# Attention and token mixer in one kernel: order of the last projection tiles, place of the row statistics, and a planner's weights

## The chip, the cores and the metric

The kernel runs on one core of a Trainium2 chip. The metric is the device time of one execution in microseconds (us). An execution that the hardware profiler recorded gives the trace; its own time is stated beside the others.

## The reference

```
x = A_x                                            # (1, 2048, 512)
g = sigmoid((x * gate_w).sum(-1, keepdims=True))
q, k, v = split of x @ wqkv into 32 heads of 16
a = softmax(q k^T * 16**-0.5) v, heads joined, @ wo
h = layernorm(x)                                   # over the 512 channels
u = gelu(h^T w1 + b1)                              # over the 2048 tokens: (512, 1792)
b = (u w2 + b2)^T                                  # (2048, 512)
return g * a + (1 - g) * b
```

All inputs and the output are float32.

## The kernel before, in words

**Products in three parts.** A float32 factor is split into a high and a low part of TensorE's reduced float32 format; a product is three matmuls (high by high, high by low, low by high). A projection tile of 512 tokens by 128 columns, or of 128 tokens by 512 columns of v, has 512 rows of weights, four blocks of 128, and so twelve matmuls of 128 x 512.

**Tiles of q and k.** There are 32 tiles, numbered T: four of 512 tokens for each block of 128 columns, key block 0 (T 0 to 3), query block 0 (T 4 to 7), key block 1 (T 8 to 11), and so on. A tile is copied from its PSUM bank to `qraw`, cut into its parts in a buffer named `pc` (a key tile two parts, a query tile three, the third with a bound of the scores), and its parts are stored to DRAM (`kp`, `qp`), all in `qk_parts`. The greatest absolute value of its columns is kept besides. For a group (a pair of heads and half of the queries) the parts are loaded back as stacks of rows: `load_k` (six transfers to `ks`, for half of the keys) and `load_q` (eight transfers to `qs`). Query tiles 4 and 5 hold the first half of the queries of block 0.

**The first stage** loads x, turns it (by TensorE for the first four row blocks of 128 tokens, by VectorE from blocks `xb` for the rest), and multiplies v tile by tile. `order` lists its v tiles as numbers and the tiles 0 to 5 of k and q as strings ("woven" among them); at place i of `order` the lists `calls`, `cuts` and `stats` say what else is issued: loads, stores, and `row_stats(t)`, which gives mean, variance and the gate's sum of 128 tokens. `last` holds what is left of the woven tile before: low part, greatest value, third part and store. `store_v` writes v to DRAM for later groups. The two `pc` buffers of this stage serve the woven tiles in turn.

**The hand-over.** Tiles 6, 7 and 8 are then multiplied alone (`tile_alone`), each in one of seven PSUM banks named `s`; the eighth bank is `dn`. With them come, on ScalarE and VectorE, the layer norm's 1 / deviation (`rs`) and the gate (`g`, `omg`) of all tokens, with a load of the activation tables for the square root and one for the exponential. A first phase of eight scores follows (`mixed`): four, tile 9 alone, four. Then the phases of twelve scores begin, the first with tile 10 alone ahead of it.

**Phases.** A score is a matmul of 64 x 128 by 64 x 512 to one bank. In a phase, scores on one half of TensorE's rows stand beside matmuls on the other half, which add up a tile of q or k (or, in the second attention part, of the mixer's second layer) in `dn`. ScalarE takes exponentials of one or two banks to `pt`; four banks of each phase are first copied to `quad` by VectorE (line 779 of the kernel before) and have one exponential together. At a phase's end the exponentials of the phase before are multiplied with v (line 839).

**The plan of banks.** `plan_banks` decides, when the program is built, in which bank each score goes. It walks the phases with estimates of each engine's time, keeps the eight best states (`WIDTH`), and orders them by `State.worth`. `kept` holds a neighbouring bank for the second score of a pair that has one exponential, with the time from which it is free. There are two plans: the mixed phase with the 42 phases of twelve scores of the first attention part, and the second attention part.

All engines' instructions stand in the order in which the code issues them, but for small moves that the scheduler makes; all transfers are issued by one queue, SP's, in order. A transfer waits until the eighth before it has landed.

Of the kernel before, what the change touches and what calls it, by code (L numbers as in the profile page):

```python
# [22 lines left out]
P = 128  # L23
# [53 lines left out]
def gated_mix(ctx: ExitStack, tc: tile.TileContext, a_x, a_wqkv, a_wo, b_w1, b_b1, b_w2, b_b2, gate_w, out):  # L77
# [129 lines left out]

    def qk_parts(T, raw, pc, alone):

        j, b, is_q, n = qk_tile(T)  # L210
        low, high = (2, 0) if is_q else (1, 0)
        if n == 0:
            (qmax if is_q else kmax)[b] = small.tile([P, NQ], F32, name="qmax" if is_q else "kmax")
# [11 lines left out]
        def first():  # L225
            (nc.scalar.copy if alone else nc.vector.tensor_copy)(pc[:, high, :], raw)

        def second():
            nc.vector.tensor_tensor(pc[:, low, :], raw, pc[:, high, :].bitcast(F32), ALU.subtract)

        def shift():
            if alone:
                nc.scalar.activation(pc[:, 1, :], raw, AF.Abs, scale=kmax[b][:, 0:1])
            else:
                most_k, other = kmax[b][:, 0:1], pc[:, 1, :].bitcast(F32)
                nc.vector.tensor_scalar(pc[:, 1, :], raw, most_k, -1.0, ALU.mult, ALU.mult)
                nc.vector.scalar_tensor_tensor(pc[:, 1, :], raw, most_k, other, ALU.mult, ALU.max)

        def store():
            dst = (qp_d if is_q else kp_d)[b]  # L240
            nc.sync.dma_start(dst[:, :, n * NB : (n + 1) * NB].rearrange("c p t -> p c t"), pc.bitcast(F32))

        return [(0.45, first), (0.7, greatest), (0.7, second), *([(1.2, shift)] if is_q else [])], store

    def parts_of(pool, T, **kw):
        return pool.tile([P, 3, NB], F32R, name="pc", **kw)[:, : 3 if qk_tile(T)[2] else 2, :]

# [21 lines left out]
    with tc.tile_pool(name="vp", bufs=1, side="right") as pool:  # L269
# [32 lines left out]
        blocks_of = {}  # L302

        def load_blocks(t):
            blocks_of[t] = pool.tile([P, QUARTERS, P], F32, name="xb", bufs=4)
# [37 lines left out]
        def store_v(t, to):  # L343
            nc.sync.dma_start(v_d[:, t:to], v[:, t:to])
# [4 lines left out]
        with tc.manual_schedule():  # L349
# [70 lines left out]
            def woven(T):  # L420
# [17 lines left out]
            def v_tile(t):  # L438
# [15 lines left out]
            cuts, late_cuts = {}, []  # L454
            stats = {**{i: [i] for i in range(10)}, 13: [10], 14: [11], 15: [12], 16: [13], 17: [14], 18: [15]}
            for i, what in enumerate(order):
# [16 lines left out]
                for call in calls.get(i, ()):  # L473
# [8 lines left out]
            store_v(12, NS)  # L482
            load_q(0)
    acc_ctx.close()
# [34 lines left out]
    TILES_PT, QUADS = 8, 2  # L519
    WIDTH = 8  # L520

# [6 lines left out]
    class State:  # L528

        def __init__(self, free):  # L530
            self.free = list(free)
# [58 lines left out]
        def score(self, n, ops, parked, u, bank, since, alone):  # L590
# [4 lines left out]
            if alone:  # L595
                at = min(range(RING), key=lambda b: new.free[b])
                new.pe = max(new.pe + TURN, new.free[at]) + ALONE_PE + TURN
                new.act = max(new.act, new.pe) + ALONE_ACT
                new.free[at] = new.act
                new.alone += ((u, at),)  # L600
# [80 lines left out]
        def worth(self):  # L681
            return self.pe + 0.02 * sum(max(0, f - self.pe) for f in self.free) + 0.1 * max(0, self.act - self.pe)

    def plan_banks(phases, free):

        best = [State(free)]
        sets = 0
# [12 lines left out]
        best = sorted((new for old in best for new in old.with_v(0, (), (), 0.0, sets)), key=State.worth)  # L700
        log, steps, free = best[0].log, [], best[0].free
# [4 lines left out]
        return deque(step[1:] for step in reversed(steps) if step[0] == "s"), v_banks, free  # L706

# [259 lines left out]
    with tc.manual_schedule(engines=engines):  # L967
        e, y, t_, w_ = (small.tile([P, NS], F32, name=f"st{n}", bufs=1) for n in range(4))
        turn_of = deque(range(RING))

        def tile_alone(T, bank):
            for n, (a, b) in enumerate(qk_pairs(T)):
                writes(nc.tensor.matmul(banks[:, bank, :], a, b, start=n == 0, stop=n == 3 * ND - 1), bank)  # L973
            raw = qe.tile([P, NB], F32, name="qraw", bufs=4)
            reads(nc.scalar.copy(raw, banks[:, bank, :]), bank)  # L975
            steps, store = qk_parts(T, raw, parts_of(qe, T, bufs=4), T < ALONE - 1)
            for n in (0, 2, 3, 1):
                if n < len(steps):
                    steps[n][1]()
            store()  # L980

        for T in range(WOVEN, ALONE - 2):
# [5 lines left out]
            tile_alone(T, turn_of[0])  # L988
            if T == WOVEN:
                nc.vector.tensor_scalar_add(w_, mv[:, :, 1], EPS)  # L990
                nc.scalar.activation(y, w_, AF.Sqrt)
                nc.scalar.activation(e, z, AF.Exp, scale=-1.0)
                nc.vector.tensor_scalar_add(e, e, 1.0)
                nc.vector.reciprocal(g, e)
                nc.vector.tensor_scalar(omg, g, -0.5, 0.5, ALU.mult, ALU.add)
            if T == WOVEN + 1:
                nc.vector.reciprocal(y, y)
                nc.vector.tensor_mul(t_, y, y)
                nc.vector.tensor_mul(t_, t_, w_)
                nc.vector.tensor_scalar(t_, t_, -0.5, 1.5, ALU.mult, ALU.add)  # L1000
                nc.vector.tensor_mul(rs, y, t_)
            if T < WOVEN + 2:
# [555 lines left out]
```

## Time and profile before

| what | value |
|---|---|
| time, median of three executions | 1256.97 us |
| the three executions | 1256.45, 1256.97, 1263.55 us |
| time of the profiled execution | 1262.87 us |
| its span, first to last instruction | 1260.0 us |
| TensorE (PE) busy | 1243.1 us, 99% |
| ScalarE (ACT) busy | 1079.3 us, 86% |
| VectorE (DVE) busy | 776.1 us, 62% |
| GpSimd (POOL) busy | 215.8 us, 17% |
| mean granted TensorE clock | 0.992 |
| first attention part, from its first score to the mixer's first layer | 78.72 to 334.94 us |
| mixer's first layer, up to the first score of the second part | to 491.87 us |

The waits of an engine are grouped by the line that waited and the instruction that ended the wait; after the colon stand the total in us, how many, and the longest. In a timeline a row is the start, the length, the engine, the line, and what is written from what; a number in brackets is the idle time ahead of it. In a table by stretches, the clock that TensorE was granted, the share of the DMA engines and GB/s stand last.

### The profile page before, as it was taken

The numbers are of one execution on the slowest core, as the hardware profiler recorded it, in microseconds if no ns is written. First come the engines' busy times: TensorE is split into PE (matmuls) and PEld (weight loads), VectorE is DVE, ScalarE is ACT, GpSimd is POOL, SyncE is SP. The second block draws the span as 40 slices with busy tenths as digits, with TensorE's granted clock in tenths as the row PEclk, the third lists the DMA queues.
The fourth block names the chain that finished last, engine by engine and source line by source line (L and its number), as shares of the span: only waits on it lengthen the run. The fifth ranks groups of instructions, "written<-read, shape, count | busy, mean of one in ns | idle before, by whom it ended". The sixth has DMA issues, their size and how long they took to land.

```text
span 1260.0 us, 33250 instructions
## 1 busy us (share of the span) xinstructions
PE 1243.1 (99%) x13446; PEld 798.8 (63%) x13446; DVE 776.1 (62%) x1318; ACT 1079.3 (86%) x1561; POOL 215.8 (17%) x345
## 2 busy tenths in 40 slices
PE   9989999999999999999999999999999999999998
PEld 7865666666678886566566556655666566555666
DVE  6747887888784347555455445545555556647974
ACT  4459999999734337999999999999999999999990
POOL 5400000000145444111111111101112111100000
PEclk9989999999999999999999999999999999999999
DMA  6882544452464433054234333324433443436642
GB/s 184 284 255 70 135 121 129 111 154 94 125 211 134 123 100 106 23 127 94 73 78 104 95 86 92 92 68 101 106 82 92 107 127 94 105 73 177 180 135 88
DMA packets 169919, 149.17 MB, mean 118 GB/s; under 512 B 82055, under 2 KB 127261, under 8 KB 169374
## 3 DMA queue, kind: packets, MB, share of 16 engines
q1 hardware_dynamic: 169758, 146.97, 42.9%
q8 instruction: 108, 1.77, 0.6%
q14 instruction: 53, 0.43, 0.1%
HBM read 108.50 MB, written 38.39 MB: 117 GB/s over the span
## 4 chain that ended last, share of the span: by engine, by line
PE 95%; ACT 2%; DMA 1%; DVE 1%; issue 0%; SPq 0%; ACTq 0%; DVEq 0%
PE s L839 36%; PE s L789 34%; PE s L1215 12%; PE dn L803 5%; PE acc L91 3%; PE pa L1434 2%; PE acc L424 1%; PE s L973 1%; DMA row<-bp 1%; ACT pt L772 1%; DMA x<-in_A_x_dram 0%; PE acc L388 0%; DVE quad L779 0%; PE dn L1434 0%; ACT qraw L975 0%
## 5 line engine op out<-in xcount | busy, mean ns | idle before, releaser
L772 ACT ACTIVATE pt<-s 128x512 f32<-128x512 f32 (+1 forms) x1217 | 717.3, 704 | 5.8 <-PE s L789 3.1
L789 PE MATMUL s<-qs,ks 64*128 64x512 f32 x2048 | 526.8, 404 | 9.1 <-DVE quad L779 2.9
L789 PEld LDWEIGHTS s<-qs,ks 64*128 64x128 f32 x2048 | 353.0, 185 | 170.6 <-ACT pt L772 74.2
L779 DVE COPY quad<-s 128x512 f32<-128x512 f32 x616 | 401.1, 687 | 52.1 <-PE dn L803 35.2
L839 PE MATMUL s<-pt,vt 128*17 128x256 f32 x5728 | 422.5, 380 | 0.0
L768 ACT ACTIVATE quad<-quad 128x2048 f32<-128x2048 f32 x154 | 300.3, 1950 | 1.3 <-DVE quad L779 1.2
L839 PEld LDWEIGHTS s<-pt,vt 128*17 128x17 f32 x5728 | 181.2, 97 | 164.9 <-ACT pt L772 53.3
L851 DVE TENSOR_TENSOR ot<-s,ot 128x256 f32<-128x256 f32 (+1 forms) x155 | 79.4, 512 | 304.6 <-PE s L839 212.9
L803 PE MATMUL dn<-u,w_hi 64*128 64x512 f32 x768 | 256.5, 407 | 0.0
L839 PE MATMUL s<-quad,vt 128*17 128x256 f32 x2464 | 226.6, 379 | 0.0
L1042 POOL TENSOR_TENSOR w_lo<-w_raw,w_hi 128x512 fp32r<-128x512 f32 (+1 forms) x127 | 149.6, 1183 | 101.6 <-ACT w_hi L1039 78.3
L808 POOL MEMSET token<- 1x1 f32 x154 | 18.0, 117 | 849.9 <-PE dn L803 772.5
L803 PE MATMUL dn<-u,w_lo 64*128 64x512 f32 x384 | 156.1, 406 | 0.0
L839 PEld LDWEIGHTS s<-quad,vt 128*17 128x17 f32 x2464 | 100.7, 98 | 60.2
L803 PEld LDWEIGHTS dn<-u,w_hi 64*128 64x128 f32 x768 | 136.5, 185 | 2.3 <-POOL token L808 0.2
L1215 PE MATMUL s<-h,w_hi 128*128 128x512 f32 x392 | 121.0, 390 | 0.0
L1039 ACT CAST w_hi<-w_raw 128x512 fp32r<-128x512 f32 (+1 forms) x64 | 36.1, 565 | 58.4 <-PE s L1215 30.3
L1215 PEld LDWEIGHTS s<-h,w_hi 128*128 128x128 f32 x392 | 73.5, 188 | 15.7 <-issue 0.4
L1215 PE MATMUL s<-h,w_lo 128*128 128x512 f32 x196 | 76.8, 392 | 0.0
L803 PEld LDWEIGHTS dn<-u,w_lo 64*128 64x128 f32 x384 | 71.0, 185 | 1.2
L803 PE MATMUL dn<-xt_hi,wc_hi 64*128 64x512 f32 x168 | 70.5, 420 | 0.0
L803 PE MATMUL dn<-xt_lo,wc_hi 64*128 64x512 f32 x168 | 65.8, 392 | 0.0
(197 smaller groups left out, 1178.2 us busy)
## 6 DMA issues: line engine op xcount, KB each, us to landing
ks<-kp SPq DMA_DIRECT2D x384, 64.0 KB
w_raw<-in_B_w_dram SPq DMA_DIRECT2D x96, 256.0 KB
qs<-qp SPq DMA_DIRECT2D x256, 64.0 KB
qp<-pc SPq DMA_DIRECT2D x16, 768.0 KB
x<-in_A_x_dram SPq DMA_DIRECT2D x32, 256.0 KB
kp<-pc SPq DMA_DIRECT2D x16, 512.0 KB
vt<-v_d SPq DMA_DIRECT2D x30, 272.0 KB
w_raw<-in_B_w_dram SPq DMA_DIRECT2D x32, 128.0 KB
```

The costliest lines, as they stand in the source:

```text
L91: nc.tensor.matmul(ps, a, b, start=start and n == 0, stop=stop and n == last)
L768: act = nc.scalar.activation(dst, dst, AF.Exp, scale=SCALE)
L772: act = nc.scalar.activation(dst, banks[:, at[0] : at[-1] + 1, :], AF.Exp, scale=SCALE)
L779: reads(nc.vector.tensor_copy(homes[op][:, op.index(u), :], banks[:, units[u][5], :]), units[u][5])
L789: mm = nc.tensor.matmul(banks[:, bank, :], kt[2 * grp + c * P // SH][rows, c * P % SH : c * P % SH + P], qt[grp][rows, qb * NB : (qb + 1) ...
L803: mm = nc.tensor.matmul(ps, a[half], b[half], start=first and not second, stop=last and bool(second))
L839: mm = nc.tensor.matmul(av[32 * j : 32 * j + VC, at : at + QC], vt[grp][:, c, i, :], pt[:, h * QC : (h + 1) * QC], start=m == 0, stop=m == ...
L851: reads(nc.vector.tensor_tensor(x, added, x, ALU.add), bank)
L1039: copy(hi, raw)
L1042: sub(lo, raw, hi.bitcast(F32), ALU.subtract)
L1215: mm = nc.tensor.matmul(banks[:, bank, :], a, h[c][:, b, :], start=c == 0 and k == 0, stop=c == NS - 1 and k == 2)
L1434: nc.tensor.matmul(pa[t], a, b, start=i == 0 and t % 2 == 0, stop=i == 3 * ND - 1)
```

## The change

1. `order`: tiles 3, 4 and 5 come ahead of v tile 12, so that all six woven tiles stand ahead of the last four v tiles. The places in `calls` move with them; `load_q(0)` now stands at the last v tile, ahead of the last store of v, and `bring_wcols(3)` (the weights of tiles 12 to 15) behind that store.
2. What is left of a woven tile (`last`) is issued ahead of the `row_stats` of its place, and the statistics of rows 11 to 15 come two at a time and later.
3. Tiles 2 and 3 put their two parts in two `xb` buffers instead of one `pc` buffer; their stores are two transfers each instead of one.
4. The layer norm's and the gate's last steps are written behind the first stage instead of among tiles 6 and 7.
5. Tile 9 is added up in `dn` instead of in one of the seven banks.
6. `plan_banks` makes a plan for each of four weights of a new term of `worth` (how long the kept banks are still taken) and takes the one whose last state ends first. With weight 0.0 the rule is the old one. In the changed program the first plan is that of weight 1.0, and the banks of its scores differ in each of its 43 phases; the second plan is that of weight 0.0, and it is the same as before, entry for entry.

```
-    def qk_parts(T, raw, pc, alone):
+    def qk_parts(T, raw, parts, alone):
...
+        pc, whole = parts
...
         def store():
-            dst = (qp_d if is_q else kp_d)[b]
-            nc.sync.dma_start(dst[:, :, n * NB : (n + 1) * NB].rearrange("c p t -> p c t"), pc.bitcast(F32))
+            dst = (qp_d if is_q else kp_d)[b][:, :, n * NB : (n + 1) * NB]
+            if whole is None:
+                for c, part in enumerate(pc):
+                    nc.sync.dma_start(dst[c], part.bitcast(F32))
+            else:
+                nc.sync.dma_start(dst.rearrange("c p t -> p c t"), whole.bitcast(F32))
...
-                steps, store = qk_parts(T, raw, parts_of(pool, T, bufs=2), True)
+                if T in (2, 3):
+                    parts = [block_tile().rearrange("p a c -> p (a c)").bitcast(F32R) for _ in range(2)], None
+                else:
+                    parts = parts_of(pool, T, bufs=2)
+                steps, store = qk_parts(T, raw, parts, True)
...
-            order = [*range(2, 12), "0", "1", "2", 12, "3", "4", "5", 13, 14, 15]
+            order = [*range(2, 12), "0", "1", "2", "3", "4", "5", 12, 13, 14, 15]
...
-                13: [lambda: store_v(8, 12)],
-                14: [lambda: cuts.update({18: bring_wcols(2)})],
-                15: [lambda: load_k(0)],
-                17: [lambda: load_k(1)],
-                19: [lambda: late_cuts.extend(bring_wcols(3))],
+                13: [lambda: cuts.update({18: bring_wcols(2)})],
+                14: [lambda: load_k(0)],
+                16: [lambda: store_v(8, 12), lambda: load_k(1)],
+                19: [lambda: load_q(0)],
             }
-            cuts, late_cuts = {}, []
-            stats = {**{i: [i] for i in range(10)}, 13: [10], 14: [11], 15: [12], 16: [13], 17: [14], 18: [15]}
+            cuts = {}
+            stats = {**{i: [i] for i in range(10)}, 15: [10], 16: [11, 12], 17: [13, 14], 18: [15]}
...
+                while last:
+                    last.pop(0)()
                 for t in stats.get(i, ()):
                     row_stats(t)
...
-                while last:
-                    last.pop(0)()
...
             store_v(12, NS)
-            load_q(0)
+            late_cuts = bring_wcols(3)
+            e, y, t_, w_ = (small.tile([P, NS], F32, name=f"st{n}", bufs=1) for n in range(4))
+            nc.vector.tensor_scalar_add(w_, mv[:, :, 1], EPS)
+            nc.scalar.activation(y, w_, AF.Sqrt)
+            nc.scalar.activation(e, z, AF.Exp, scale=-1.0)
...
-    WIDTH = 8
+    WIDTH, WEIGHTS = 8, (0.0, 0.1, 0.3, 1.0)
...
             if alone:
-                at = min(range(RING), key=lambda b: new.free[b])
-                new.pe = max(new.pe + TURN, new.free[at]) + ALONE_PE + TURN
+                at = None if u else min(range(RING), key=lambda b: new.free[b])
+                new.pe = max(new.pe + TURN, 0.0 if u else new.free[at]) + ALONE_PE + TURN
...
         def worth(self):
-            return self.pe + 0.02 * sum(max(0, f - self.pe) for f in self.free) + 0.1 * max(0, self.act - self.pe)
+            waits = sum(max(0.0, since - self.pe - SLOT) for _, since in self.kept.values())
+            return self.pe + self.weight * waits + 0.02 * sum(max(0, f - self.pe) for f in self.free) + 0.1 * max(0, self.act - self.pe)

     def plan_banks(phases, free):

-        best = [State(free)]
+        phases = list(phases)
+        return min((plan_of(phases, free, weight) for weight in WEIGHTS), key=lambda found: found[0])[1:]
+
+    def plan_of(phases, free, weight):
+
+        best = [State(free, weight)]
...
         def tile_alone(T, bank):
+            ps = ps_dn.tile([P, D], F32, name="dn") if bank is None else banks[:, bank, :]
...
             tile_alone(T, turn_of[0])
-            if T == WOVEN:
-                nc.vector.tensor_scalar_add(w_, mv[:, :, 1], EPS)
-                nc.scalar.activation(y, w_, AF.Sqrt)
-                nc.scalar.activation(e, z, AF.Exp, scale=-1.0)
...
```

Three places in the engines' orders. The queue of transfers, SP, from the store of tile 3's parts to the stores of tiles 6 and 7 (`kp` and `qp` are the parts in DRAM, `wc_raw` weights of q and k, `v_d` v in DRAM), before and then after:

```order
L344 DMA v_d<-v 128x2176
L150 DMA wc_raw<-in_A_wqkv_dram 128x4x128
L241 DMA kp_65<-pc 128x2x512
L170 DMA ks_88<-kp_65 16x1024 x6
L241 DMA qp_60<-pc 128x3x512 x2
L170 DMA ks_89<-kp_65 16x1024 x6
L150 DMA wc_raw<-in_A_wqkv_dram 128x4x128
L344 DMA v_d<-v 128x2176
L170 DMA qs_91<-qp_60 16x1024 x8
L241 DMA qp_60<-pc 128x3x512 x2
```

```order
L150 DMA wc_raw<-in_A_wqkv_dram 128x4x128
L244 DMA kp_65<-xb 128x512 x2
L170 DMA ks_88<-kp_65 16x1024 x6
L246 DMA qp_60<-pc 128x3x512
L281 DMA x<-in_A_x_dram 128x512
L246 DMA qp_60<-pc 128x3x512
L353 DMA v_d<-v 128x2176
L170 DMA ks_89<-kp_65 16x1024 x6
L170 DMA qs_91<-qp_60 16x1024 x8
L353 DMA v_d<-v 128x2176
L150 DMA wc_raw<-in_A_wqkv_dram 128x4x128
L246 DMA qp_60<-pc 128x3x512 x2
```

The eight loads of the query stack moved ahead of the last store of v and of a load of weights; the second store of v moved behind the stores of tiles 4 and 5.

ScalarE at the end of the first stage, from the last copy of v to the parts of tile 6 (`st` are the statistics of all tokens, `z` the gate's sums), before and then after:

```order
L347 COPY v<-dn 128x32x16
L975 COPY qraw<-s 128x512
L226 CAST pc<-qraw 128x512
L233 ACTIVATE pc<-qraw,kmax 128x512
L991 ACT_TABLE_LOAD
L991 ACTIVATE st_865<-st_867 128x16
L992 ACT_TABLE_LOAD
L992 ACTIVATE st_864<-z 128x16
```

```order
L356 COPY v<-dn 128x32x16
L1008 COPY qraw<-s 128x512
L498 ACT_TABLE_LOAD
L498 ACTIVATE st_832<-st_834 128x16
L499 ACT_TABLE_LOAD
L499 ACTIVATE st_831<-z 128x16
L227 CAST pc<-qraw 128x512
L234 ACTIVATE pc<-qraw,kmax 128x512
```

The square root and the exponential of the statistics moved ahead of the parts of tile 6, but stay behind the copy of it.

ScalarE again, in the mixed phase, from its first exponentials to the copy of tile 10, before and then after:

```order
L772 ACTIVATE pt<-s 128x512 x2
L772 ACTIVATE pt<-s 128x1024
L975 COPY qraw<-s 128x512
L226 CAST pc<-qraw 128x512
L772 ACTIVATE pt<-s 128x1024 x2
L975 COPY qraw<-s 128x512
```

```order
L803 ACTIVATE pt<-s 128x512 x2
L803 ACTIVATE pt<-s 128x1024
L1008 COPY qraw<-dn 128x512
L227 CAST pc<-qraw 128x512
L803 ACTIVATE pt<-s 128x1024 x2
L1008 COPY qraw<-s 128x512
```

The order is the same; the copy of tile 9 now reads `dn`.

More of the change, by code (lines that the diff above doesn't have):

```diff
@@ L302, in gated_mix, with block_tile @@
         blocks_of = {}
+        def block_tile():
+            return pool.tile([P, QUARTERS, P], F32, name="xb", bufs=4)
         def load_blocks(t):
-            blocks_of[t] = pool.tile([P, QUARTERS, P], F32, name="xb", bufs=4)
+            blocks_of[t] = block_tile()
             src = xf[t * P : (t + 1) * P, :].rearrange("(a r) (q c) -> q r a c", r=BLOCK, q=QUARTERS)
@@ L528, in gated_mix, with __init__ @@
     class State:
-        def __init__(self, free):
-            self.free = list(free)
+        def __init__(self, free, weight):
+            self.free, self.weight = list(free), weight
             self.pe = self.act = self.dve = 0.0
@@ L595, in score @@
             if alone:
-                at = min(range(RING), key=lambda b: new.free[b])
-                new.pe = max(new.pe + TURN, new.free[at]) + ALONE_PE + TURN
+                at = None if u else min(range(RING), key=lambda b: new.free[b])
+                new.pe = max(new.pe + TURN, 0.0 if u else new.free[at]) + ALONE_PE + TURN
                 new.act = max(new.act, new.pe) + ALONE_ACT
-                new.free[at] = new.act
+                if not u:
+                    new.free[at] = new.act
                 new.alone += ((u, at),)
@@ L705, in plan_banks @@
         v_banks = deque(step[1] for step in reversed(steps) if step[0] == "v")
-        return deque(step[1:] for step in reversed(steps) if step[0] == "s"), v_banks, free
+        return end, deque(step[1:] for step in reversed(steps) if step[0] == "s"), v_banks, free
     planned, v_banks = deque(), deque()
@@ L967, in gated_mix @@
     with tc.manual_schedule(engines=engines):
-        e, y, t_, w_ = (small.tile([P, NS], F32, name=f"st{n}", bufs=1) for n in range(4))
         turn_of = deque(range(RING))
         def tile_alone(T, bank):
+            ps = ps_dn.tile([P, D], F32, name="dn") if bank is None else banks[:, bank, :]
             for n, (a, b) in enumerate(qk_pairs(T)):
-                writes(nc.tensor.matmul(banks[:, bank, :], a, b, start=n == 0, stop=n == 3 * ND - 1), bank)
+                mm = nc.tensor.matmul(ps, a, b, start=n == 0, stop=n == 3 * ND - 1)
+                if bank is not None:
+                    writes(mm, bank)
             raw = qe.tile([P, NB], F32, name="qraw", bufs=4)
-            reads(nc.scalar.copy(raw, banks[:, bank, :]), bank)
+            copy = nc.scalar.copy(raw, ps)
+            if bank is not None:
+                reads(copy, bank)
             steps, store = qk_parts(T, raw, parts_of(qe, T, bufs=4), T < ALONE - 1)
```

34 lines of the change are left out of this document (17 added, 17 removed).

## The prediction

> **What bounds the kernel now.** I read the page first: the shares by engine and the row of the granted clock.
>
> ```profile
> PE 1243.1 (99%) x13446; PEld 798.8 (63%) x13446; DVE 776.1 (62%) x1318; ACT 1079.3 (86%) x1561; POOL 215.8 (17%) x345
> PEclk9989999999999999999999999999999999999999
> ```
>
> TensorE is the bound nearly everywhere, so an edit pays only where TensorE waits or runs slowly. The clock has its one visible dip in the third slice of 31.5 us, which holds the hand-over from the projections to the attention. The waits of TensorE, first from 66 to 106 us, then in the rest of the first attention part (106 to 344 us), say the same:
>
> ```profile
> PE s L789 <- DMA qs<-qp: 1.5, 1, 1.5
> PE s L789 <- ACT qraw L975: 1.4, 2, 0.7
> PE s L789 <- ACT pt L772: 0.9, 1, 0.9
> PE s L789 <- DVE quad L779: 0.7, 1, 0.7
> PE s L789 <- ACT pc L226: 0.6, 1, 0.6
> ```
>
> ```profile
> PE s L1215 <- DVE hu L1073: 0.5, 1, 0.5
> ```
>
> So 5.1 us of waits lie in the hand-over and 0.5 us in the 238 us behind it. The timeline of TensorE at the hand-over (start, length, what; idle time before it in brackets), and then the granted clock (the number behind POOL's busy time, ahead of the DMA share) in three stretches:
>
> ```profile
> 74.36 0.39 PE L973 MATMUL s<-xt_hi,wc_hi 128*128 128x512 f32 x1
> ...
> 76.86 0.39 PE L973 MATMUL s<-xt_hi,wc_lo 128*128 128x512 f32 x1
> 78.72 0.47 PE L789 MATMUL s<-qs,ks 64*128 64x512 f32 x1 [1.48 <-DMA qs<-qp]
> 79.84 1.19 PE L789 MATMUL s<-qs,ks 64*128 64x512 f32 x3 [0.65 <-ACT pc L226]
> 80.96 0.79 PE L973 MATMUL s<-xt_hi,wc_hi 128*128 128x512 f32 x1
> ...
> 85.82 0.63 PE L973 MATMUL s<-xt_hi,wc_lo 128*128 128x512 f32 x1
> 87.12 0.72 PE L789 MATMUL s<-qs,ks 64*128 64x512 f32 x3 [0.68 <-ACT qraw L975]
> 88.74 0.49 PE L789 MATMUL s<-qs,ks 64*128 64x512 f32 x1 [0.90 <-ACT pt L772]
> 89.16 0.50 PE L973 MATMUL s<-xt_hi,wc_hi 128*128 128x512 f32 x1
> ...
> 93.38 0.40 PE L973 MATMUL s<-xt_hi,wc_lo 128*128 128x512 f32 x1
> 94.45 0.49 PE L789 MATMUL s<-qs,ks 64*128 64x512 f32 x1 [0.68 <-ACT qraw L975]
> ...
> 96.83 0.50 PE L789 MATMUL s<-qs,ks 64*128 64x512 f32 x1 [0.72 <-DVE quad L779]
> ```
>
> ```profile
> 81.00:83.00 2.00, 2.00 (x6) 1.61 (x6) 1.93 (x4) 1.69 (x3) 0.00 (x0) 0.50 1.05 373
> 90.00:93.00 3.00, 3.00 (x9) 2.32 (x8) 0.00 (x0) 0.29 (x1) 0.00 (x0) 0.50 1.03 228
> 500.00:505.00 5.00, 4.26 (x18) 2.23 (x18) 2.18 (x4) 5.00 (x10) 0.00 (x0) 0.50 0.18 52
> ```
>
> Twelve matmuls of a tile stand between the first and the last row of each tile. Tile 8 takes (76.86 - 74.36) / 11 = 0.227 us a matmul, 2.73 us a tile; tile 9 (80.96 to 85.82) 0.442, 5.30; tile 10 (89.16 to 93.38) 0.384, 4.60. The idle time is followed by a halved clock, and that costs 2.57 + 1.87 = 4.4 us beside the waits.
>
> **The change part by part.** *The order of tiles.* Tiles 3 to 5 run one v tile earlier, 2.73 us; v tile 12 takes their place; TensorE's work is the same. What matters is when the query stack of the first group has landed. A row of ScalarE's timeline (the cast of tile 5), and then rows of the issuing queue:
>
> ```profile
> 64.34 0.62 ACT L226 CAST pc<-qraw 128x512 fp32r<-128x512 f32 x1 [2.28 <-DMA kp<-pc]
> ```
>
> ```profile
> 64.05 2.10 SPq L241 DMA_DIRECT2D qp<-pc  x2
> 66.20 4.07 SPq L170 DMA_DIRECT2D ks<-kp  x6
> 70.37 0.55 SPq L150 DMA_DIRECT2D wc_raw<-in_A_wqkv_dram  x1
> 71.01 0.56 SPq L344 DMA_DIRECT2D v_d<-v  x1
> 71.63 5.85 SPq L170 DMA_DIRECT2D qs<-qp  x8
> ```
>
> Before, the store of tile 5's parts ends its issue at 66.15, the last `qs` is issued at 77.48, and its last readers start at 79.84, so landing takes up to 2.36 us. After, tile 5 ends 2.73 us earlier, and its first part no longer waits those 2.28 us for a `pc` buffer, since tiles 2 and 3 write `xb` buffers; the store is then issued about 66.15 - 2.73 - 2.28 = 61.1. Behind it stand one store of v (0.56), six `ks` (4.07) and eight `qs` (5.85): 71.6, landed by 74.0. TensorE wants it at 76.86 + 0.23 = 77.1, a margin of 3.1 us. The third store of v and a load of weights now stand behind `qs`. They start near 72; the store (1,088 KB) took from 71.01 to about 77 before, since the last `qs` waited 0.7 us for it:
>
> ```profile
> SPq L170 <- DMA v_d<-v: 0.7, 1, 0.7
> ```
>
> So it lands about 78. The first exponential writes memory that v held and needs that landing at 79.75 (next paragraph), a margin of 1.7 us. The split store of tiles 2 and 3 is two more issues of about 0.5 us on a queue that waits there anyway: nothing.
>
> *Row statistics and the gate.* On VectorE the rows' statistics of tokens 10 to 15 go behind the parts, which only moves work that TensorE doesn't wait for. The square root and the exponential go ahead of the parts of tile 6 on ScalarE. That is a swap inside a stretch that ScalarE fills:
>
> ```profile
> 71.96 0.59 ACT L975 COPY qraw<-s 128x512 f32<-128x512 f32 x1 [2.25 <-PE s L973]
> ...
> 73.85 1.28 ACT L991 ACT_TABLE_LOAD   x1
> ...
> 75.36 1.28 ACT L992 ACT_TABLE_LOAD   x1
> ...
> 79.13 0.62 ACT L226 CAST pc<-qraw 128x512 fp32r<-128x512 f32 x1
> 80.69 2.00 ACT L772 ACTIVATE pt<-s 128x512 f32<-128x512 f32 x3 [0.94 <-PE s L789]
> ...
> 86.48 0.59 ACT L975 COPY qraw<-s 128x512 f32<-128x512 f32 x1 [3.79 <-PE s L973]
> ...
> 87.66 1.02 ACT L772 ACTIVATE pt<-s 128x1024 f32<-128x1024 f32 x1
> ```
>
> ScalarE is done with tile 8 at 79.13 + 0.62 = 79.75 in either order. That cover holds as long as nobody needs tile 6's parts early; they are queries of the second half, so nobody does. Cost: nothing.
>
> *The tenth tile in another bank, and the gap closed.* Now the walk of both engines after. TensorE: four scores from 77.1 at 0.23 us, 78.0; tile 9 in `dn` at once, 78.1 to 80.8. ScalarE: three exponentials 79.75 to 81.7 (2.00), copy and first part of tile 9 to 82.9 (1.18, from 86.48 to 87.66), two exponentials of two banks (1.02 each) to 84.9. The next scores take banks of the first two exponentials, free at about 80.3 and 80.8 (0.5 us a bank), so TensorE issues them 80.9 to 81.9, then tile 10 to 84.7; its result is there at 84.9. Both engines arrive together; the copy of tile 10 (0.64 us from its start to the score behind it, as the copy's row below against 94.45) ends the stretch:
>
> ```profile
> 93.81 0.59 ACT L975 COPY qraw<-s 128x512 f32<-128x512 f32 x1 [3.52 <-PE s L973]
> ```
>
> The first score of the twelve comes at 84.9 + 0.64 = 85.5 against 94.45: **8.9 us**. Of these 4.4 are the clock, 4.5 the waits and the order of ScalarE and TensorE. If the idle time goes, so should the halved clock. What is late next is the same chain as before, copy of tile 10, VectorE's copies to `quad`, the score that waits 0.72 us at 96.83; it moves along.
>
> *The plan of banks.* The second plan is the same entry for entry: nothing in the second attention part. The first changes the banks of all 42 phases of twelve scores. There is hardly anything to gain: a phase is 5.7 us,
>
> ```profile
> 138.47 2.72 PE s L839 x48
> 144.14 2.71 PE s L839 x48
> ```
>
> (144.14 - 138.47 = 5.67 between the last products of two phases), of which twelve scores at 0.227 are 2.72 and the products with v another 2.72, and from 106 to 344 us only 0.5 us is waited. What it may lose is a rival below; I take 0, bounds +0.7 us of gain (the wait at 96.83) and 0.72 us of loss for each phase that gets such a wait.
>
> Sum against the profiled execution, 1262.87 us (span 1260.0 and 2.87 around it): 1262.87 - 8.9 = 1254.0. The three timed executions are 1256.45, 1256.97 and 1263.55, so the profiled one lies 5.9 us over the median. Nothing else in the trace could differ that much between executions but the halved clock, 4.4 us here, and the stretch at 500 us. If the median execution kept its clock at the hand-over, only 4.5 us are left to gain: 1256.97 - 4.5 = **1252.5**. If it didn't, 1256.97 - 8.9 = 1248.1.
>
> [...]
>
> **The rivals.** *The clock was slow in the median execution too* (1248.1). For it: the idle pieces of 1.48 and 0.65 us lie in each execution. Against it: the 5.9 us then have no place in the trace.
>
> *The data stay late.* If `qs`, or the store of v ahead of the first exponential, slips by its margin and as much again, the first scores start near 78.7 as before. The DMA engines are almost full there (shares of 1.05 and 1.03 in the first two stretches above). Then only the 1.5 us or so of bank waits go: 1256.97 - 1.5 = 1255.5, and at worst nothing.
>
> *The new banks wait* (the slower side). Each phase of twelve scores places them in other banks; where one comes free later than assumed, TensorE waits about the 0.72 us of the row at 96.83. Seven of 42 phases (7 x 0.72 = 5.0) eat the 4.5 us; half of them give 1252.5 + 21 x 0.72 = 1267.6, all of them 1282.7. Against it: VectorE and ScalarE do the same work in each phase, and the old banks cost nothing.
>
> **How the numbers follow.** Forecast 1252.5 us, chance 0.50; slow clock in the median execution, 1248.1, 0.24; late data, 1255.5, 0.13; new banks that wait, 1258 to 1283, 0.08; more than the sum, by waits I don't see, 0.05. The range takes in the first three: 1247 (1248.1 less the 0.7 us and the 0.5 us between the two lower timed executions) to 1257 (no gain). About 1% is what a measurement of this kernel tells from no change: under 1244.4 needs 3.7 us beyond the largest sum, 0.04; over 1269.5 needs 24 of 42 phases with a wait, 0.03; within, 0.93.
>
> **What would show it.** Right: no idle row ahead of the first score, a clock of 1.00 from 77 to 94 us, tile 9 in 2.7 us, the first score of the twelve near 85.5, phases still 5.7 us, the same times from there to the second plan less 8.9. Wrong: an idle row with `qs` or a store of v as its releaser; a clock of 0.50 without an idle row; a gap between products with v above 5.75 us; or a hand-over shorter by 8.9 us with a time that hasn't moved.

## The result, and the profile after

| | before | after |
|---|---|---|
| median time, us (ten executions each) | 1261.28 (1256.45 to 1264.21) | 1253.72 (1252.96 to 1255.39) |
| ratio, with 95% interval | | 0.9946 (0.9929 to 0.9962) |
| profiled execution, us | 1262.87 | 1254.86 |
| its span, us | 1260.0 | 1253.1 |
| its mean granted clock | 0.992 | 0.996 |

The changed kernel is 0.4 to 0.7% faster, so the time lies in the range and within the 1%. The ten executions of the kernel before include the three that the prediction had; their median is 4.3 us above that of the three. In the experiments below, three executions of 2466 to 6020 us (two of the kernel before, one of e9) are left out of every median.

The page of the changed kernel, the shares by engine and the row of the granted clock. The dip of the third slice is gone; the one in the sixteenth slice (470 to 501 us) is the start of the second attention part.

```profile
PE 1239.8 (99%) x13446; PEld 795.6 (63%) x13446; DVE 775.9 (62%) x1318; ACT 1079.0 (86%) x1561; POOL 214.8 (17%) x345
PEclk9999999999999998999999999999999999999999
```

TensorE's waits of the changed kernel from 66 to 96 us (line, what ended the wait, total, number, longest). Of 5.1 us in five rows, 1.4 us in two are left, the two that the walk had kept:

```profile
PE s L820 <- DVE quad L810: 0.7, 1, 0.7
PE s L820 <- ACT qraw L1008: 0.7, 1, 0.7
```

The timeline of TensorE at the hand-over of the changed kernel. No idle time stands ahead of the first four scores, tile 9 (`dn`) takes 77.51 to 80.46, and the first score of the twelve starts at 84.82; the walk had 85.5, the kernel before 94.45.

```profile
76.53 0.39 PE L1004 MATMUL s<-xt_hi,wc_lo 128*128 128x512 f32 x1
76.85 0.73 PE L820 MATMUL s<-qs,ks 64*128 64x512 f32 x4
77.51 0.50 PE L1004 MATMUL dn<-xt_hi,wc_hi 128*128 128x512 f32 x1
...
80.46 0.73 PE L820 MATMUL s<-qs,ks 64*128 64x512 f32 x4
81.12 0.50 PE L1004 MATMUL s<-xt_hi,wc_hi 128*128 128x512 f32 x1
...
83.76 0.39 PE L1004 MATMUL s<-xt_hi,wc_lo 128*128 128x512 f32 x1
84.82 0.50 PE L820 MATMUL s<-qs,ks 64*128 64x512 f32 x1 [0.68 <-ACT qraw L1008]
...
87.20 0.50 PE L820 MATMUL s<-qs,ks 64*128 64x512 f32 x1 [0.72 <-DVE quad L810]
```

From the last matmul of tile 8 to this score are 84.82 - 76.53 = 8.29 us, and were 94.45 - 76.86 = 17.59: the hand-over is 9.3 us shorter. The queue of transfers and ScalarE of the changed kernel show what feeds it:

```profile
58.33 0.41 SPq L246 DMA_DIRECT2D qp<-pc  x1
...
59.95 0.83 SPq L246 DMA_DIRECT2D qp<-pc  x1
60.83 0.64 SPq L353 DMA_DIRECT2D v_d<-v  x1
61.52 5.87 SPq L170 DMA_DIRECT2D ks<-kp  x6
67.43 3.93 SPq L170 DMA_DIRECT2D qs<-qp  x8
71.46 0.37 SPq L353 DMA_DIRECT2D v_d<-v  x1
```

```profile
79.18 1.99 ACT L803 ACTIVATE pt<-s 128x512 f32<-128x512 f32 x3
81.05 0.59 ACT L1008 COPY qraw<-dn 128x512 f32<-128x512 f32 x1
...
82.20 1.93 ACT L803 ACTIVATE pt<-s 128x1024 f32<-128x1024 f32 x2
84.18 0.58 ACT L1008 COPY qraw<-s 128x512 f32<-128x512 f32 x1
```

The last `qs` is issued by 71.4 (walk: 71.6), and ScalarE runs from the exponentials to the copy of tile 10 with no gap over 0.1 us. The clock of the changed kernel in two stretches (the 1.00 and 0.66 behind POOL's busy time), and of the kernel before in its own:

```profile
80.00:90.00 10.00, 8.60 (x59) 5.01 (x61) 7.27 (x12) 8.39 (x13) 0.09 (x1) 1.00 1.00 270
490.00:500.00 10.00, 8.67 (x54) 3.95 (x56) 4.03 (x8) 10.00 (x15) 2.10 (x3) 0.66 0.09 28
```

```profile
80.00:90.00 10.00, 8.43 (x23) 5.28 (x24) 4.11 (x10) 4.91 (x7) 0.00 (x0) 0.67 0.68 225
90.00:100.00 10.00, 8.60 (x62) 5.55 (x64) 4.29 (x7) 4.96 (x9) 0.09 (x1) 0.83 0.67 167
```

Below, *lead* is by how much a kernel's products with v start earlier than the same products of the kernel before in its profiled execution. The changed kernel leads by 9.39 us at the first products, 8.65 at 318 us, 7.41 behind the start of the second attention part at 506 us, and 6.9 at the end of the span. The other 1.1 us of the 8.0 between the two profiled times lie outside the spans (2.87 and 1.76 us); the section on the phases of twelve shows which part of the change they go with.

### The profile page after: what moved, and what is told of

Same layout as the page of the kernel before. It is cut to its first block, busy times and chain, and to the rows that moved or that the text cites. A ratio compares the mean times of both kernels' runs of the same rounds, so it can differ in the third digit from the quotient of the medians.

```text
span 1253.1 us, 33344 instructions
## 1 busy us (share of the span) xinstructions
PE 1239.8 (99%) x13446; PEld 795.6 (63%) x13446; DVE 775.9 (62%) x1318; ACT 1079.0 (86%) x1561; POOL 214.8 (17%) x345
## 4 chain that ended last, share of the span: by engine, by line
PE 90%; DVE 3%; DMA 2%; SPq 2%; issue 1%; ACT 1%; POOL 0%; DVEq 0%; ACTq 0%
PE s L820 36%; PE s L870 36%; PE s L1237 11%; PE dn L834 3%; PE pa L1456 2%; DMA xb<-in_A_x_dram 1%; PE s L1004 1%; DMA row<-bp 1%; DVE xw L322 1%; PE acc L433 1%; PE acc L91 1%; SPq L170 1%; DMA gw<-in_gate_w_dram 1%; DVE hf L1087 0%; DVE h L1095 0%
```

## The experiments

The kernel before ran beside every group of experiments: 1260.78 us (29 executions) in the first four, 1260.88 (27) in the next four, 1261.87 (11) in the last four. Each time is a median; the first score of the twelve, the waits and the clock are those of one profiled execution.

### One part undone, one part alone

*The plan of banks undone* in the changed kernel (e1):

```
-    WIDTH, WEIGHTS = 8, (0.0, 0.1, 0.3, 1.0)
+    WIDTH, WEIGHTS = 8, (0.0,)
```

> The changed kernel with the one weight 0.0, so that the plan of banks is made by the old rule (with the tenth tile still in dn). My theory, that the new plan is worth nothing between the hand-over and the mixer's first layer: 1253.7 us, within 0.7 us of the changed kernel, and the first score of the twelve at 84.8 us as there. Rival, the new plan takes waits away: 2 to 4 us slower than the changed kernel, with waits for a bank between 95 and 330 us. Second rival, the new plan costs the 0.7 us by which the changed kernel's lead shrank between 89 and 326 us: about 1253.0.

1256.83 us, ratio 0.9972 (0.9962 to 0.9983), about 3 us of the gain lost, first score of the twelve at 87.02 (84.82 in the changed kernel). My theory fell. TensorE's timeline of this kernel has the place, and ScalarE's beside it the cause:

```profile
80.08 0.73 PE L820 MATMUL s<-qs,ks 64*128 64x512 f32 x3
82.89 0.50 PE L820 MATMUL s<-qs,ks 64*128 64x512 f32 x1 [2.09 <-ACT pt L803]
87.02 0.50 PE L820 MATMUL s<-qs,ks 64*128 64x512 f32 x1 [0.68 <-ACT qraw L1008]
```

```profile
81.82 1.02 ACT L803 ACTIVATE pt<-s 128x1024 f32<-128x1024 f32 x1
```

In the mixed phase the old rule puts the eight scores in banks 0, 1, 4, 5, 0, 1, 2, 1, the new one in 0, 1, 4, 5, 0, 1, 2, 3. By the old rule the eighth score writes the bank of the sixth, so it waits for the exponential that reads it (82.84); TensorE is idle for 2.09 us, and tile 10 behind it is late by as much.

*The plan of banks alone* in the kernel before (the new term of `worth`, nothing else; e2):

```
+            waits = sum(max(0.0, since - self.pe - SLOT) for _, since in self.kept.values())
...
+        return min((plan_of(phases, free, weight) for weight in WEIGHTS), key=lambda found: found[0])[1:]
```

> The kernel before with the new rule of the plan alone. My theory: the time of the kernel before, 1256.5 to 1264.2 us with a median near 1261, ratio 1.000 within 0.002, the first score of the twelve at 94.4 us. Rival, the plan carries a part of the gain: ratio 0.998 or less. Rival, it costs: ratio 1.001 or more, and the lead of the phases over the kernel before shrinks between 95 and 330 us.

1257.72 us, ratio 0.9979 (0.9968 to 0.9991): 3 us by itself. The wait of the eighth score, 0.90 us in the kernel before, is gone, its second four scores start together at 85.13, and the first score of the twelve comes at 89.50:

```profile
85.13 0.73 PE L795 MATMUL s<-qs,ks 64*128 64x512 f32 x4 [0.68 <-ACT qraw L981]
89.50 0.50 PE L795 MATMUL s<-qs,ks 64*128 64x512 f32 x1 [0.68 <-ACT qraw L981]
```

In this profiled execution the clock lost 1.7 us at the hand-over where the record of the kernel before lost 5.2, so of the 4.95 us between 94.45 and 89.50 the larger part is clock.

*The tenth tile in `dn` alone* in the kernel before (e5), and *undone* in the changed kernel (e4):

```
-                at = min(range(RING), key=lambda b: new.free[b])
+                at = None if u else min(range(RING), key=lambda b: new.free[b])
...
+            ps = ps_dn.tile([P, D], F32, name="dn") if bank is None else banks[:, bank, :]
```

> The kernel before with the tenth tile in dn alone, planned by the old rule. My theory: with the old rule the eighth score still gets the bank of the sixth and waits for its exponential, as in the first experiment, so the first score of the twelve stays near 94.4 us and the time near the kernel before's 1260.8. Rival, the wait of 0.7 us for the copy of tile 9 goes with the bank: 0.7 us earlier, and up to 2.5 us if tile 10 then keeps its clock.

> The changed kernel with the tenth tile (tile 9) in one of the seven banks again, planned by the new rule. My theory: the score behind it waits for the copy of tile 9, which ScalarE reaches at 81.05 us behind three exponentials, so the four scores start at 81.7 instead of 80.46 us; of these 1.2 us about 1.0 reach the first score of the twelve (85.8 instead of 84.8): 1254.7 us. If that idle time halves the clock for tile 10, 2 us more. Rival, another bank is free and nothing is lost: 1253.7.

Alone 1261.62 us, ratio 1.0005 (0.999 to 1.0019): nothing. The second four scores no longer wait there for the copy of tile 9 (0.68 us before), but by the old rule the eighth of them then waits longer for its bank, 1.59 us against 0.90. The wait has moved:

```profile
PE s L790 <- DMA qs<-qp: 2.6, 2, 1.8
PE s L790 <- ACT pt L773: 1.6, 1, 1.6
```

Undone in the changed kernel 1254.2 us, ratio 0.9953 (0.9937 to 0.9968), with a wait of 1.16 us for ScalarE's copy of tile 9 ahead of the second four scores and the first score of the twelve at 86.03, 1.2 us later.

```profile
81.63 0.74 PE L819 MATMUL s<-qs,ks 64*128 64x512 f32 x4 [1.16 <-ACT qraw L1007]
```

With the rest in place the bank saves that wait; against the changed kernel's 1253.72 it is a difference that these intervals don't separate.

*The order of tiles without the plan and without the bank* (the changed kernel with the lines of e1 and of e4 undone; e7):

> The changed kernel with the old rule of the plan and the tenth tile in one of the seven banks: order of tiles and place of the statistics alone. My theory: no wait for the stack, but 1.2 us for the copy of tile 9 and about 1 us for an exponential ahead of the eighth score; the first score of the twelve near 87.5 us, 1257 us, 3 to 4 us under the kernel before. Rival, the order alone carries the whole gain: 1254; rival, it carries nothing without the new plan: 1260.8.

1256.53 us, ratio 0.9967 (0.9953 to 0.998): 4.4 us. First score of the twelve at 88.62, 1.1 us later than expected; the waits were those I had named (1.17 us for the copy, 0.89 for the exponential), but the clock fell behind them:

```profile
84.00:93.00 9.00, 7.60 (x43) 5.03 (x45) 4.13 (x7) 3.97 (x7) 0.09 (x1) 0.81 0.78 255
```

(1 - 0.81) x 9 = 1.7 us of lost clock. The times add up within their intervals: order alone 4.4, plan alone 3.1, bank alone nothing, together 7.6 us.

*The query stack behind the last store of v* in the changed kernel (e6):

```
-                19: [lambda: load_q(0)],
...
             late_cuts = bring_wcols(3)
+            load_q(0)
```

> The changed kernel with the load of the query stack behind the last store of v and the load of weights again, all else as changed. My theory: the last transfers of the stack wait for that store, the stack lands about 78.2 us, TensorE idles about 1.3 us ahead of the first scores; the first score of the twelve at 86.1 us if the clock stays at 1.00, up to 88 if it falls: 1255 to 1257 us. Rival, the order of the tiles alone brings the stack in time: 1253.7.

1256.17 us, ratio 0.9968 (0.9954 to 0.9982), first score of the twelve at 86.49. TensorE's timeline shows the two waits that this place of the load causes:

```profile
77.11 0.47 PE L820 MATMUL s<-qs,ks 64*128 64x512 f32 x1 [0.69 <-DMA qs<-qp]
78.55 0.70 PE L820 MATMUL s<-qs,ks 64*128 64x512 f32 x3 [0.97 <-DMA qs<-qp]
```

They are 1.66 us; the median says 2.5. Here the clock stayed at 1.00.

### The parts costed at nothing

Each of these undoes one part of the changed kernel. The statistics back among tiles 6 and 7 (e9), the parts of tiles 2 and 3 back in `pc` buffers (e10), and the changed kernel once more as their measure (e11):

```
+            if T == WOVEN:
+                nc.vector.tensor_scalar_add(w_, mv[:, :, 1], EPS)
+                nc.scalar.activation(y, w_, AF.Sqrt)
...
```

```
-                if T in (2, 3):
-                    parts = [block_tile().rearrange("p a c -> p (a c)").bitcast(F32R) for _ in range(2)], None
-                else:
-                    parts = parts_of(pool, T, bufs=2)
+                parts = parts_of(pool, T, bufs=2)
```

> The changed kernel with the statistics of the second load back among its parts (only that part of the change undone). My theory, as in the prediction: in that stretch ScalarE is filled either way and ends at the same time, so the swap of two pieces of its work is worth nothing: 1253.7 us, first score of the twelve at 84.8 us as in the changed kernel. Rival: the swap lets the query parts land earlier and pays for part of the gain: some 0.5 to 1 us more, and a TensorE wait for qs of a few tenths ahead of tile 9.

> The changed kernel with tiles 2 and 3 of the query back in the two pc buffers (only that part of the change undone). My theory, as in the prediction: the query's second stack then waits some 2.3 us for a buffer, and qs lands near 76 us in place of 74, still ahead of the first score at 77: 1253.7 us, first score of the twelve at 84.8, at most 0.5 us more. Rival: the later parts push the key and query tiles behind TensorE's need; TensorE then waits for qs and its clock falls: about 1256 us.

> The changed kernel itself, once more, as the measure for the three others on the same chip: 1253.7 us, 7 us under the kernel before, first score of the twelve at 84.8 us.

1253.23 us, ratio 0.9937 (0.9924 to 0.9949), without the statistics' move; 1253.06, 0.9936 (0.9924 to 0.9949), with two `pc` buffers; 1253.01, 0.9932 (0.9919 to 0.9944), for the changed kernel: no difference that these intervals tell apart. The first score of the twelve came at 84.16, 84.32 and 85.56; they differ because whole executions are shifted by up to 1.4 us already at the end of tile 8, and the stretch from the first four scores to this one is 7.97 to 7.98 us in all three (84.16 - 76.19, 84.32 - 76.35, 85.56 - 77.58). In e10 the casts of tiles 4 and 5 wait for the store of the buffer, as they did before:

```profile
57.76 0.62 ACT L227 CAST pc<-qraw 128x512 fp32r<-128x512 f32 x1 [1.78 <-DMA kp<-pc]
60.76 0.62 ACT L227 CAST pc<-qraw 128x512 fp32r<-128x512 f32 x1 [1.29 <-DMA kp<-pc]
```

The query stack is issued 1.6 us later (68.98 against 67.43) and TensorE doesn't wait for it. The `xb` buffers buy margin, not time.

### The clock by itself

Eleven matmuls whose result nobody reads, put into the idle time of the kernel before ahead of its first score (e3):

```
+        unread = ps_dn.tile([P, D], F32, name="dn")
+        for n in range(11):
+            nc.tensor.matmul(unread, qk_w[2][0][:, 0, :], xt_hi[:, 0, 0:NB], start=n == 0, stop=n == 10)
```

> The kernel before with eleven matmuls more between tile 8 and the first score, whose result in dn nobody reads; they fill 2.5 us of the time in which TensorE waits for the query stack, and change no wait. My theory, the idle time there brings the halved clock: tiles 9 and 10 take 2.7 us each instead of 5.3 and 4.6, the first score of the twelve comes at 90.0 us instead of 94.45, the profiled span is 4.4 us shorter; if the later idle pieces of 0.7 and 0.9 us halve the clock again for tile 10, 2.6 us shorter. Its slowest executions should be gone, and the median be 3 to 5 us under that of the kernel before. Rival, the clock falls for another reason (the transfers, the exponentials): clock 0.50 from 80 to 86 us as before, the same time or up to 0.3 us slower.

In the trace it came out as expected. The other waits are still there, the clock is 1.00 from 77 to 93 us, and the first score of the twelve comes at 89.72 (expected 90.0; 94.45 before):

```profile
80.00:84.00 4.00, 3.32 (x17) 2.21 (x14) 2.21 (x4) 2.64 (x5) 0.00 (x0) 1.00 1.05 334
84.00:93.00 9.00, 6.72 (x36) 4.43 (x38) 4.56 (x8) 4.97 (x8) 0.00 (x0) 1.00 0.79 227
```

So the idle time ahead of the first score is what halves the clock (0.50 from 79.69 to 86.52 us in the kernel before), and not in this trace alone: the mean granted clock of the twelve executions is 0.9965 on average, against 0.9945 for the 29 of the kernel before beside them, which would be 2.5 us. But the median of the twelve is 1259.42 us, ratio 0.9994 (0.9982 to 1.0006): 1.4 us by the medians, with no difference excluded, where the pair of traces shows 4.7. The execution of the kernel before that was profiled lost more clock than most (its mean is 0.992); where the rest of the 2.5 us goes is not shown.

### The plan in the phases of twelve

From the second to the forty-first group of products (39 gaps), in the chains of waits of the changed kernel and of its repetition:

```profile
94.53 2.72 PE s L870 x48
...
317.96 2.71 PE s L870 x48
```

```profile
95.27 2.71 PE s L870 x48
...
318.69 2.71 PE s L870 x48
```

223.43 and 223.42 us, or 5.73 a gap. The same stretch takes 222.8 us in the kernel before and 222.2 with the old rule (e1). With tile 9 in one of the seven banks it takes 223.3 by the new plan (e4) and 222.4 by the old (e7); in the kernel before the new plan (e2) costs nothing, 222.6. One cause is in the chain of the changed kernel: VectorE's sum of finished products (`ot`) ends the wait of a score for its bank, and TensorE starts 0.28 us late.

```profile
176.57 1.18 issue
177.75 0.70 DVE ot L882
178.46 0.04 issue
178.50 0.50 PE s L820
```

So the new plan helps in the mixed phase and, in the changed kernel, costs behind it. A kernel with the new weight in the first phase alone has the new bank for the eighth score and the old rule's banks in the rest (e8, and e12 once more):

```
             best = [new.close(blocks) for new in best]
+            for new in best:
+                new.weight = 0.0
```

> The changed kernel with the new term of the plan in its first phase alone; from the second phase on the weight is 0.0, so the 42 phases of twelve scores are planned by the old rule, and of the mixed phase only the bank of the eighth score differs from the old rule's. My theory: what the plan is worth lies in that one bank: first score of the twelve at 84.8 us as in the changed kernel, and a lead that doesn't shrink up to 326 us, 1253.0 us, 0.7 us under the changed kernel. Rival, the plan is worth its 3 us in the 42 phases: 1256.8 as with the old rule.

> The changed kernel with the new weight in the first phase alone, once more beside the changed kernel on the same chip. My theory: the first phase's one bank is the whole worth of the new plan and the later phases pay 0.7 us for it: 0.7 to 0.8 us under the changed kernel, so 1252.9 to 1253.0, with a lead that doesn't shrink in the first part. Rival: what was seen was the noise of executions, and the two are equal within 0.3 us.

The stretch is shorter in both records, 222.31 and 222.43 us:

```profile
94.39 2.71 PE s L872 x48
...
316.70 2.71 PE s L872 x48
```

```profile
94.40 2.71 PE s L872 x48
...
316.83 2.71 PE s L872 x48
```

And its first score of the twelve comes at 84.75 in both, so what the plan gains at the hand-over is that one bank. The first run gave 1252.91 us, ratio 0.9939 (0.9918 to 0.9959), the second, beside the changed kernel's 1253.01, gave 1253.47, 0.9936 (0.9923 to 0.9949). The 0.8 us that I expected of the second run did not come, as the rival had it.

The spans of the same executions show why. A program's time is its span and a part outside it, and that part goes with the plan: in all 55 executions of the programs whose phases of twelve have the new plan (changed, e2, e4, e6, e9, e10) it is 1.73 to 1.91 us, in all 126 of those with the old rule's banks there (before, e1, e3, e5, e7, e8 with e12) 2.40 to 3.14. No run shows the reason. By the medians:

| kernel | executions | time, us | span, us |
|---|---|---|---|
| changed, with its repetition | 15 | 1253.50 | 1251.60 |
| new weight in the first phase alone (e8, e12) | 11 | 1252.92 | 1250.20 |
| old rule (e1) | 12 | 1256.83 | 1254.05 |

The one bank takes 3.9 us off the span (e1 against e8 and e12), of which some 0.9 is clock by the mean clocks (0.9959 and 0.9966). The new plan of the other phases adds 1.4 to the span, and with it the part outside the span is 1.0 shorter, so that little of what it costs reaches the time. Each kernel's executions spread over more than 3 us; I call no version better than the changed kernel.

## Why the prediction was right, and where it wasn't

**The place and the walk were right.** The gain comes from the hand-over: 9.3 us in the traces against the sum's 8.9. The walk was 0.7 us late at the first score of the twelve, because four scores took 0.66 us (76.85 to 77.51) and not 0.91, as two run on the two halves of TensorE's rows at once (the four start in pairs, two near 76.85 and two near 77.18), and ScalarE was done with tile 8 at 79.27, not 79.75. What is late next is the chain that was named: copy of tile 10, `quad`, a wait of 0.72 us.

**Order of tiles: right.** TensorE doesn't wait for `qs`, nor ScalarE for a store of v; with the load behind the store of v, TensorE waits twice for `qs` again and the time rises by 2.5 us. The 2.28-us wait that tiles 2 and 3 free was right as a mechanism, but it only widens a margin that is wide enough without it.

**Statistics: right**, nothing either way.

**The failed step: the plan of banks at 0.** The walk let the second four scores follow each other in banks that were free. That is so only by the new plan, so its worth stood in the sum of 8.9 already, under "the tenth tile in another bank, and the gap closed", while the text gave the plan nothing. Measured, the plan is worth about 3 us, of which some 2 lie in the span (1254.05 against 1251.90 for the ten executions of the changed kernel) and 1.0 outside it, where the sum had no term; and the bank `dn` at most 1.2 us in the trace and nothing alone. I had looked for waits in the 42 phases, and the row that the plan removes, 0.90 us for an exponential at 88.74, stood in the mixed phase and in the quoted rows. In the phases behind it the plan costs: gaps of 5.82, 6.08, 6.00 and 5.86 us in the changed kernel, four above the 5.75 that I had named as a sign, where the kernel before has two (6.06 and 5.83). That is the rival of the waiting banks, at 0.7 us of lead, not the 5 us that would have decided it.

**The forecast's own step, "only 4.5 us are left to gain": half right.** It took 1256.97 us as the typical time of the kernel before. Its first case (A) was that this execution kept its clock, so that 4.5 us of waits and order are left and 0 of clock; its other case (B) was that it didn't, and 4.4 us of clock come on top. The measured gain is 7.6 us, from a base 4.3 us higher. The 67 later executions of the kernel before, by their mean granted clock:

| mean granted clock | executions | median us |
|---|---|---|
| 0.992 | 9 | 1262.02 |
| 0.993 | 9 | 1262.62 |
| 0.994 | 16 | 1261.66 |
| 0.995 | 18 | 1259.50 |
| 0.996 | 9 | 1258.02 |
| 0.997 | 6 | 1257.92 |

The executions do differ by the clock, as case A had it. But the one at 1256.97 is among the fastest of them (three of 67 lie below it), and the median execution, 1260.98, has a low clock. At an equal clock the size of case A's term comes out: the six executions at 0.997 have a median of 1257.92, the ten of the changed kernel at 0.997 one of 1253.38, which is 4.5 us. Only 3.6 of them lie in the span (1255.10 and 1251.55), where the sum had its waits and its order; the other 1.0 lies outside it, so the agreement is partly luck. The rest of the 7.6, some 3 us, is clock: (0.9971 - 0.9944) x 1255 = 3.4 us by the mean clocks of 15 and 67 executions. So the clock term is, by this estimate, 3 us in a typical execution, between the 0 of case A and the 4.4 of case B. The forecast hit the time because a base that was too low and a gain that was too small made up for each other. The sum against the profiled execution, 1254.0, stands 0.9 us from the changed kernel's profiled 1254.86, and there too errors offset: 2.5 us of the lead are lost behind the hand-over (9.39 to 6.9), and 1.1 are gained outside the span.

**Not foreseen:** of the 9.39 us of lead at the first products, 0.7 go in the phases and 1.2 at the start of the second attention part, where the clock is slow in every trace, whatever the kernel, and the loss differs from one execution to the next (1.7 to 5.1 us from 490 to 510 us). Nor was the 1.0 us by which the part outside the span is shorter with the new plan.

## What to carry to other kernels

When a chain is walked through by hand, write beside each step which edit makes it possible; a sum can be right while its parts are credited to the wrong edits, and then undoing one of them surprises. A wait that a planner removes may lie in the one odd phase rather than in the many equal ones, so look for its row there first. Before a time is predicted from a profiled execution and a few timed ones, find out by the mean granted clock which of them is typical; a base that is 4 us off weighs as much as the change.

## What the runs showed of the hardware that was not expected

The clock that is lost, (1 - granted clock) x length over stretches of 10 us, comes in steps of about 1.7 us:

| kernel | 70 to 100 us | 490 to 510 us |
|---|---|---|
| before | 5.2 | 3.4 |
| after, and once more | 0, 0 | 3.4, 3.4 |
| old rule (e1) | 0 | 5.1 |
| plan alone (e2) | 1.7 | 3.4 |
| clock kept (e3) | 0 | 5.1 |
| bank undone (e4) | 0 | 3.5 |
| bank alone (e5) | 3.4 | 1.7 |
| query behind v (e6) | 0 | 3.4 |
| order alone (e7) | 1.7 | 3.4 |
| first phase alone (e8, e12) | 0, 0 | 1.7, 3.4 |
| statistics back (e9), two buffers (e10) | 0, 0 | 3.4, 1.7 |

A step is what one fall of the kernel before loses: 3.41 us at a clock of 0.50, from 89.94 to 93.35 us.

The length of an idle piece alone doesn't decide whether a step is lost: the clock stayed at 1.00 behind 2.09 us (e1), behind 1.16 us (e4) and behind 0.69 and 0.97 us close together (e6), and fell behind 1.48 and 0.65 us (before) and behind 1.17 and 0.89 us (e7), all in single records.

What does separate the cases is in the traces. Wherever the clock falls at the hand-over or at 490 us in the 14 traces, it is 0.50 for 3.41, 6.83 or 10.24 us, and where a trace has several falls their starts lie a whole number of stretches of 3.413 us apart (in the kernel before 79.69 and 499.53: 123 of them). So each trace is divided here into such stretches, counted on from a fall in both directions; that borders lie so where no fall stands is an assumption. Counted so, the borders don't go by the program's start: in two executions of the changed kernel there is one at 76.32 in the first (its fall starts at 492.75), and at 78.08 us in the second. TensorE's idle time in some of the stretches:

| kernel | stretch, us | idle, us | clock in it | clock in the next |
|---|---|---|---|---|
| before | 76.28 to 79.69 | 1.98 | 1.00 | 0.50 |
| before | 86.52 to 89.94 | 1.50 | 1.00 | 0.50 |
| order alone (e7) | 80.65 to 84.07 | 1.52 | 1.00 | 0.50 |
| two buffers (e10) | 83.31 to 86.72 | 1.40 | 1.00 | 1.00 |
| old rule (e1) | 78.37 to 81.78 | 0.97 | 1.00 | 1.00 |
| old rule (e1) | 81.78 to 85.20 | 1.12 | 1.00 | 1.00 |

From 74 to 96 us in all 14 traces, the six stretches ahead of a fall hold 1.50 to about 2.2 us of idle time, and every other one at full clock holds at most 1.40. So at the hand-over it is the sum of the idle time in one stretch that separates the two; the 2.09 us of e1 lie across a border. In the kernel before, 1.50 of 3.41 us in sum was enough. No run was made to try this. At 490 us it doesn't hold: the fall came behind 1.05 us of idle time in the kernel before (496.12 to 499.53) and behind 1.56 in the changed kernel (489.34 to 492.75). What decides there, and why some falls last two or three stretches, stays open.
